# Storing dK, dV and o of an attention backward kernel in other pieces

## The chip, the cores and the metric

The kernel runs on one NeuronCore of a Trainium2 chip. Its engines are TensorE (PE in the profile), VectorE (DVE), ScalarE (ACT), GpSimd (POOL) and SyncE (SP), each with an instruction queue of its own, and sixteen DMA engines move data between the device memory and SBUF. The metric is the device time of one execution in microseconds (us), as the median of several runs. All times are of the whole kernel unless a part is named.

## The reference

Grouped query attention with its gradients, for 32 batches, 32 query heads of 4 positions, 4 key heads of 2048 positions and 128 elements, all bfloat16. The forward pass and its vector-Jacobian product are returned: o, dq, dk and dv.

```python
def _fwd_reference(q, k, v):
    B, Hq, Sq, D = q.shape
    Hkv = k.shape[1]
    rep = Hq // Hkv
    k = jnp.repeat(k, rep, axis=1)
    v = jnp.repeat(v, rep, axis=1)
    scale = D ** -0.5
    scores = jnp.einsum("bhqd,bhkd->bhqk", q, k) * scale
    p = _softmax(scores, axis=-1)
    return jnp.einsum("bhqk,bhkd->bhqd", p, v)

def reference(q, k, v, grad_out):
    ...
    _out, _vjp = jax.vjp(_f, q, k, v)
    _grads = _vjp(grad_out)
    _out0 = jnp.asarray(_out)
    return (_out0, *[jnp.asarray(_g) for _g in _grads])
```

For each batch k and v are 2 MB each and are read once; dk and dv are 2 MB each and are written once. o, dq, q and grad_out are 32 KB a batch.

## The kernel before

One batch is the unit of work. Its 32 query heads by 4 positions are 128 rows, which fill the 128 partitions, 32 rows for each of the four key heads. Key position 16p + c of a head lies in partition p at place c, so that each partition reads and writes 4 KB in one piece for each head.

The steps of a batch, by the names that the code uses in its order lists:

- LK and LV load k and v, four DMAs of 512 KB each, on SP's queue (lines 154 and 160). Every fourth batch LK also loads q and grad_out for the next four batches, two DMAs of 128 KB, on POOL's queue (line 142, `GROUP`).
- KT and VT transpose k and v on PE (line 181), DVE copies the result out of PSUM (line 183). QDT does the same for q and grad_out.
- Sa and Sb are the scores (line 198) with their row maximum on DVE (line 211). EXa and EXb are the exponentials on ACT (line 222).
- NRM makes the reciprocal of the row sums, and POOL scales grad_out and q by it into the tiles dop and qp, eight small instructions (line 231).
- ET and dST transpose the exponentials and the score gradients (lines 248 and 250). dPa and dPb are the gradient of the probabilities (DVE, line 338).
- O and dQ gather their product over all keys in PSUM (line 264). DVE scales o (line 274) into an o tile, which is stored from POOL's queue (line 276); DVE then reads the tile again for delta (line 279). ACT scales dq (line 288), and POOL's queue stores it (line 290).
- dV and dK are outer products, eight pieces each. PE makes a piece (line 303), ACT copies it into the 2 MB tile of its batch (line 307), and after the eighth piece POOL's queue stores the tile in two DMAs of 1 MB, heads 0 and 1 and then heads 2 and 3 (line 326). The last batch is stored in halves of the keys instead, one after every four pieces (line 319).

The order of all steps is written out by hand (`HEAD`, `STEADY` and `TAIL`): steps of neighbouring batches are interleaved, `dV7@3` being piece 7 of dV of batch 3. The order holds for each engine's queue: an instruction that waits holds all behind it on its engine. In one round of `STEADY` POOL meets, in this order: dop and qp of the batch (in NRM), the store of dq of the batch before, the store of dk of the batch before, the store of o, every fourth batch the two loads for q and grad_out, and the store of dv.

Tiles come from pools with a fixed number of buffers, and a step that takes a buffer waits until the work on its last content has ended. The pools that matter here: `k_pool` 3 and `v_pool` 2 batches, `out_pool` 4 tiles shared by dk and dv, `io_pool` 3 buffers each for the o tile and the dq tile.

Of the kernel before, what the change touches and what calls it, by code (L numbers as in the profile page):

```python
# [9 lines left out]
BF16 = mybir.dt.bfloat16  # L10
ACT = mybir.ActivationFunctionType
ALU = mybir.AluOpType
# [69 lines left out]
def kernel(ctx: ExitStack, tc: tile.TileContext, q, k, v, grad_out, out_0, out_1, out_2, out_3):  # L82
    nc = tc.nc
    B, Hq, Sq, D = q.shape
    NH, Sk = k.shape[1], k.shape[2]
    P = 128
# [3 lines left out]
    scale = float(D) ** -0.5  # L90
# [11 lines left out]
    ds_pool = ctx.enter_context(tc.tile_pool(name="dsp", bufs=2))  # L102
    dst_pool = ctx.enter_context(tc.tile_pool(name="dstp", bufs=2))
    out_pool = ctx.enter_context(tc.tile_pool(name="outp", bufs=4))
    io_pool = ctx.enter_context(tc.tile_pool(name="iop", bufs=3))
    qd_pool = ctx.enter_context(tc.tile_pool(name="qdp", bufs=2))
    sm_pool = ctx.enter_context(tc.tile_pool(name="smp", bufs=3))
    ps_pool = ctx.enter_context(tc.tile_pool(name="ps", bufs=1, space=bass.MemoryType.PSUM))
# [16 lines left out]
    o_f = out_0.rearrange("b h s d -> b (h s) d")  # L125
# [6 lines left out]
    store = nc.gpsimd  # L132
    st = {}
# [125 lines left out]
    def gathered(S, xt, kv):  # L259
        t = banks.take(1)  # L260
        ps = banks.ap(t)[:, 0, 0:D]
        for c in range(C):
            for h in range(NH):
                nc.tensor.matmul(  # L264
                    ps[G * h:G * h + G, :], lhsT=S[f"{xt}{c // 8}"][:, c % 8, G * h:G * h + G], rhs=S[kv][:, h, c, :],
                    start=(c == 0), stop=(c == C - 1), tile_position=(0, G * h),
                )
        return t, ps

    def O(b):  # L270
        S = st[b]
        t, ps = gathered(S, "et", "v")
        o_sb = io_pool.tile([P, D], BF16, name="o_sb")
        nc.vector.tensor_scalar(out=o_sb[:], in0=ps, scalar1=S["rinv"][:], scalar2=None, op0=ALU.mult)
        banks.give(t)
        store.dma_start(out=o_f[b], in_=o_sb[:])
        junk = sm_pool.tile([P, D], BF16, name="junk")
        S["delta"] = sm_pool.tile([P, 1], FP32, name="delta")
        nc.vector.tensor_tensor_reduce(
            out=junk[:], in0=o_sb[:], in1=S["do"], scale=1.0, scalar=0.0,  # L280
            op0=ALU.mult, op1=ALU.add, accum_out=S["delta"][:],
        )

# [8 lines left out]
    def outer(S, x, y, dst, name, i, b, copy):  # L292

        if name not in S:
            S[name + "left"] = 8
            S[name] = out_pool.tile([P, NH, C, D], BF16, name=name, tag="outp")
        t = banks.take(2)
        ps = banks.ap(t).rearrange("p a (j c d) -> p a j c d", j=2, c=2)
        for c in range(2):
            u = P * ((2 * i + c) % 8)  # L300
            for a in range(2):
                r = slice(2 * G * a, 2 * G * a + 2 * G)
                nc.tensor.matmul(  # L303
                    ps[:, a, :, c, :], lhsT=S[f"{x}{i // 4}"][r, u:u + P], rhs=S[y][r, :, :],
                    start=True, stop=True, tile_position=(2 * G * a, 0),
                )
        copy(  # L307
            out=S[name][:, :, 2 * i:2 * i + 2, :].rearrange("p h c d -> p h (c d)"),
            in_=banks.ap(t).rearrange("p a (j w) -> p (a j) w", j=2),
        )  # L310
        banks.give(t)
        S[name + "left"] -= 1
        if b == B - 1:

            half = f"{name}half{i // 4}"
            S[half] = S.get(half, 4) - 1
            if S[half] == 0:
                c = slice(8 * (i // 4), 8 * (i // 4) + 8)
                store.dma_start(
                    out=dst[b].rearrange("p h (c d) -> p h c d", d=D)[:, :, c, :].rearrange("p h c d -> p h (c d)"),  # L320
                    in_=S[name][:, :, c, :].rearrange("p h c d -> p h (c d)"),
                )
        elif S[name + "left"] == 0:
            o = S.pop(name)
            for a in range(2):
                store.dma_start(out=dst[b][:, 2 * a:2 * a + 2, :], in_=o[:, 2 * a:2 * a + 2].rearrange("p h c d -> p h (c d)"))  # L326

    def dV(b, i, copy=nc.scalar.copy):
        outer(st[b], "e", "dop", dv_v, "dv", i, b, copy)

    def dK(b, i, copy=nc.scalar.copy):
        outer(st[b], "ds", "qp", dk_v, "dk", i, b, copy)

    def dP(b, i):
# [6 lines left out]
        banks.give(t)  # L341

    table = {"LK": LK, "LV": LV, "QDT": QDT, "O": O, "dQ": dQ, "NRM": NRM}
    for i, c in enumerate("ab"):
        for n, f in (("S", S_), ("EX", EX), ("dP", dP), ("ET", ET), ("dST", dST)):
# [8 lines left out]
    for w in STEADY.split():  # L354
        ahead = 0
        for mark, n in (("+3", 3), ("+2", 2), ("+", 1), ("-2", -2), ("-", -1)):
            if w.endswith(mark):
                w, ahead = w[:-len(mark)], n
# [3 lines left out]
    with tc.manual_schedule():  # L362

        for w in HEAD.split():
            w, b = w.split("@")
# [5 lines left out]
        for w in TAIL.split():  # L371
            w, b = w.split("@")
# [31 lines left out]
```

## Time and profile before

| what | value |
|---|---|
| time, median of 3 runs | 699.42 us (697.81 to 702.17) |
| the profiled execution, its own time | 698.71 us |
| its span from first to last instruction | 696.7 us |
| mean granted TensorE clock | 0.98 |
| PE busy | 626.0 us, 90% |
| DVE busy | 584.5 us, 84% |
| ACT busy | 569.1 us, 82% |
| POOL busy | 302.7 us, 43% |
| moved by DMA | 274.44 MB, mean 394 GB/s |
| dv, dk stores | 64 and 64 DMAs of 1 MB, 23.6 and 22.1 us from issue to landing (median) |
| o, dq stores | 32 and 32 DMAs of 32 KB, 23.2 and 16.2 us |
| k, v loads | 128 and 128 DMAs of 512 KB, 13.8 and 18.6 us |

The page of a profile describes one execution, so its sums are made against that execution's own time. A share of busy time is a mean over the whole span. The DMA row gives for each fortieth of the span the mean busy share of the sixteen DMA engines in tenths, so that a 9 can be anything from 90% on. The chain of waits follows the work back from the last instruction to what released it, at every step; the table of waits sums the time in which an engine stood still, by what ended it. A DMA has landed when all sixteen DMA engines have marked their share of it as done, and what waits for a DMA waits for the last of these marks.

### The profile page before, as it was taken

The numbers are of one execution on the slowest core, as the hardware profiler recorded it, in microseconds if no ns is written. First come the engines' busy times: TensorE is split into PE (matmuls) and PEld (weight loads), VectorE is DVE, ScalarE is ACT, GpSimd is POOL, SyncE is SP. The second block draws the span as 40 slices with busy tenths as digits, with TensorE's granted clock in tenths as the row PEclk, the third lists the DMA queues.
The fourth block names the chain that finished last, engine by engine and source line by source line (L and its number), as shares of the span: only waits on it lengthen the run. The fifth ranks groups of instructions, "written<-read, shape, count | busy, mean of one in ns | idle before, by whom it ended". The sixth has DMA issues, their size and how long they took to land.

```text
span 696.7 us, 28064 instructions
## 1 busy us (share of the span) xinstructions
PE 626.0 (90%) x12352; PEld 454.1 (65%) x12352; DVE 584.5 (84%) x992; ACT 569.1 (82%) x673; POOL 302.7 (43%) x506
## 2 busy tenths in 40 slices
PE   5899999999998989979999798998998889998982
PEld 4577776677676656666666676667766677666661
DVE  5999999999997998869988688888988869898960
ACT  0698989899887989869888687887888868888994
POOL 1355443555454435443354424544434543345452
PEclk9999999999999999999999899999999989999997
DMA  9989999999999999999999999999999999999767
GB/s 339 400 317 411 417 415 416 416 413 415 417 415 417 414 417 416 417 409 412 415 415 413 373 397 398 400 410 382 416 416 417 415 340 393 415 414 415 289 257 274
DMA packets 75577, 274.44 MB, mean 394 GB/s; under 512 B 8448, under 2 KB 8448, under 8 KB 75456
## 3 DMA queue, kind: packets, MB, share of 16 engines
q0 software_dynamic: 37536, 138.16, 49.3%
q1 hardware_dynamic: 37920, 134.50, 48.9%
q8 instruction: 96, 1.57, 0.8%
q14 instruction: 25, 0.20, 0.1%
HBM read 136.31 MB, written 136.31 MB: 391 GB/s over the span
## 4 chain that ended last, share of the span: by engine, by line
PE 43%; DMA 33%; ACT 6%; DVE 5%; POOL 5%; issue 5%; SPq 0%; POOLq 0%; DVEq 0%; ACTq 0%
PE banks L181 18%; DMA k_sb<-in_k_dram 15%; DMA out_dram<-dk 12%; PE banks L303 10%; PE banks L264 7%; ACT dv L307 5%; PE banks L248 5%; DMA out_dram<-dv 4%; PE banks L198 3%; POOL dop L231 2%; DMA v_sb<-in_v_dram 2%; DVE kt L183 2%; DVE ds L338 1%; ACT dk L307 1%; POOL qp L231 1%
## 5 line engine op out<-in xcount | busy, mean ns | idle before, releaser
L307 ACT CAST dv<-banks 128x1024 bf16<-128x1024 f32 x256 | 245.5, 1028 | 56.9 <-PE banks L303 56.3
L307 ACT CAST dk<-banks 128x1024 bf16<-128x1024 f32 x256 | 250.7, 1025 | 34.5 <-PE banks L303 23.6
L183 DVE COPY kt<-banks 128x1024 bf16<-128x1024 bf16 x256 | 164.3, 680 | 8.3 <-PE banks L181 8.3
L183 DVE COPY vt<-banks 128x1024 bf16<-128x1024 bf16 x256 | 166.2, 680 | 1.3 <-PE banks L181 0.9
L181 PE MATMUL banks<-ident,k_sb 128*128 128x128 bf16 x2048 | 145.8, 221 | 13.1 <-DMA k_sb<-in_k_dram 8.6
L181 PE MATMUL banks<-ident,v_sb 128*128 128x128 bf16 x2048 | 143.5, 220 | 14.3 <-ACT dv L307 9.7
L231 POOL TENSOR_SCALAR dop<-do_sb,rinv 32x128 bf16<-32x128 bf16 x128 | 76.7, 599 | 181.3 <-PE banks L303 118.9
L181 PEld LDWEIGHTS <-k_sb 128*128 128x128 bf16 x2048 | 120.8, 99 | 41.9 <-issue 31.7
L181 PEld LDWEIGHTS <-v_sb 128*128 128x128 bf16 x2048 | 122.2, 98 | 28.7 <-issue 23.3
L303 PE MATMUL banks<-dop,e 64*128 64x256 bf16 x1024 | 99.3, 276 | 15.1 <-POOL dop L231 11.3
L326 POOL DMA_DIRECT2D out_dram<-dv x62 | 43.7, 709 | 138.0 <-ACT dv L307 67.6
L338 DVE SCALAR_TENSOR_TENSOR ds<-banks,delta,e 128x1024 bf16<-128x1024 f32 x64 | 82.2, 1284 | 17.3 <-PE banks L198 14.3
L303 PE MATMUL banks<-qp,ds 64*128 64x256 bf16 x1024 | 86.4, 272 | 2.1 <-ACT dk L307 1.4
L231 POOL TENSOR_SCALAR qp<-q_sb,srinv 32x128 bf16<-32x128 bf16 x128 | 78.1, 610 | 10.7
L222 ACT ACTIVATE e<-banks,negb 128x1024 bf16<-128x1024 f32 x64 | 70.7, 1111 | 8.6 <-DVE negb L214 8.5
L211 DVE TENSOR_REDUCE m<-banks 128x1 f32<-128x1024 f32 x64 | 75.1, 1215 | 0.9 <-PE banks L198 0.9
L303 PEld LDWEIGHTS <-e 64*128 64x128 bf16 x1024 | 34.0, 94 | 63.1 <-issue 46.7
L250 DVE COPY et<-banks 128x1024 bf16<-128x1024 bf16 x64 | 41.3, 686 | 29.6 <-PE banks L248 29.6
L303 PEld LDWEIGHTS <-ds 64*128 64x128 bf16 x1024 | 42.2, 94 | 28.8 <-ACT dv L307 13.1
L326 POOL DMA_DIRECT2D out_dram<-dk x62 | 44.0, 713 | 13.6 <-DMA out_dram<-dk 13.0
L250 DVE COPY dst<-banks 128x1024 bf16<-128x1024 bf16 x64 | 43.5, 681 | 5.5 <-PE banks L248 3.6
L248 PE MATMUL banks<-ident,ds 128*128 128x128 bf16 x512 | 39.4, 221 | 7.1 <-ACT dk L307 6.8
(39 smaller groups left out, 484.1 us busy)
## 6 DMA issues: line engine op xcount, KB each, us to landing
k_sb<-in_k_dram SPq DMA_DIRECT2D x128, 512.0 KB, 13.8
v_sb<-in_v_dram SPq DMA_DIRECT2D x128, 512.0 KB, 18.6
out_dram<-dv POOLq DMA_DIRECT2D x64, 1024.0 KB, 23.6
out_dram<-dk POOLq DMA_DIRECT2D x64, 1024.0 KB, 22.1
out_dram<-o_sb POOLq DMA_DIRECT2D x32, 32.0 KB, 23.2
out_dram<-dq_sb POOLq DMA_DIRECT2D x32, 32.0 KB, 16.2
q_sb<-in_q_dram POOLq DMA_DIRECT2D x7, 128.0 KB, 21.9
do_sb<-in_grad_out_dram POOLq DMA_DIRECT2D x7, 128.0 KB, 22.0
```

Of the source, the lines that this page charges most:

```text
L181: nc.tensor.transpose(out=ps[:, 4 * hh + j, :], in_=S[which][:, 2 * (i % 2) + hh, 4 * (i // 2) + j, :], identity=ident[:])
L183: nc.vector.tensor_copy(out=S[f"{which}t{i}"][:], in_=ps)
L211: nc.vector.reduce_max(out=S["m"][:, i:i + 1], in_=S[f"s{i}"][1], axis=AX.X)
L222: nc.scalar.activation(out=S[f"e{i}"][:], in_=ps, func=ACT.Exp, bias=S["negb"][:], scale=scale, accum_out=S["l"][:, i:i + 1],)
L231: nc.gpsimd.tensor_scalar(out=t[r, h % 2, :], in0=src[r, :], scalar1=by[r, :], scalar2=None, op0=ALU.mult)
L248: nc.tensor.transpose(out=ps[:, u, :], in_=S[f"{src}{i}"][:, P * u:P * u + P], identity=ident[:])
L250: nc.vector.tensor_copy(out=S[f"{name}{i}"][:], in_=ps)
L264: nc.tensor.matmul(ps[G * h:G * h + G, :], lhsT=S[f"{xt}{c // 8}"][:, c % 8, G * h:G * h + G], rhs=S[kv][:, h, c, :], start=(c == 0), stop ...
L303: nc.tensor.matmul(ps[:, a, :, c, :], lhsT=S[f"{x}{i // 4}"][r, u:u + P], rhs=S[y][r, :, :], start=True, stop=True, tile_position=(2 * G * ...
L307: copy(out=S[name][:, :, 2 * i:2 * i + 2, :].rearrange("p h c d -> p h (c d)"), in_=banks.ap(t).rearrange("p a (j w) -> p (a j) w", j=2),)
L326: store.dma_start(out=dst[b][:, 2 * a:2 * a + 2, :], in_=o[:, 2 * a:2 * a + 2].rearrange("p h c d -> p h (c d)"))
L338: nc.vector.scalar_tensor_tensor(out=S[f"ds{i}"][:], in0=ps, scalar=S["delta"][:], in1=S[f"e{i}"][:], op0=ALU.subtract, op1=ALU.mult,)
```

## The change

Five edits, all on stores that POOL issues:

- dk and dv of a batch are stored in one DMA of 2 MB instead of two of 1 MB. The last batch is stored as before.
- dv of batches 3, 7, 11 and so on to 27 is stored in two DMAs instead, partitions 0 to 119 and 120 to 127.
- The o tile holds two batches, and both are stored together after the second one. The pairs that end with batch 7, 11 and so on to 31 are stored in two DMAs, partitions 0 to 103 and 104 to 127.
- The pair of batches 0 and 1 is stored in three DMAs: partitions 8 to 127 of batch 0, partitions 8 to 127 of batch 1, and partitions 0 to 7 of both.
- `io_pool` has 2 buffers instead of 3: two o tiles of two batches each, and two dq tiles.

Bytes, arithmetic and the order of the steps stay.

```diff
-    io_pool = ctx.enter_context(tc.tile_pool(name="iop", bufs=3))
+    io_pool = ctx.enter_context(tc.tile_pool(name="iop", bufs=2))
...
     def O(b):
         S = st[b]
         t, ps = gathered(S, "et", "v")
-        o_sb = io_pool.tile([P, D], BF16, name="o_sb")
-        nc.vector.tensor_scalar(out=o_sb[:], in0=ps, scalar1=S["rinv"][:], scalar2=None, op0=ALU.mult)
-        banks.give(t)
-        store.dma_start(out=o_f[b], in_=o_sb[:])
+        if b % 2 == 0:
+            st["o"] = io_pool.tile([P, 2, D], BF16, name="o_sb")
+        o_sb = st["o"][:, b % 2, :]
+        nc.vector.tensor_scalar(out=o_sb, in0=ps, scalar1=S["rinv"][:], scalar2=None, op0=ALU.mult)
+        banks.give(t)
+        if b == 1:
+            for w in range(2):
+                store.dma_start(out=o_f[w, 8:P], in_=st["o"][8:P, w])
+        if b % 2:
+            for r in (slice(0, 8),) if b == 1 else (slice(0, 104), slice(104, P)) if b % 4 == 3 and b > 3 else (slice(0, P),):
+                store.dma_start(out=o_f[b - 1:b + 1, r].rearrange("w p d -> p w d"), in_=st["o"][r])
...
         elif S[name + "left"] == 0:
-            o = S.pop(name)
-            for a in range(2):
-                store.dma_start(out=dst[b][:, 2 * a:2 * a + 2, :], in_=o[:, 2 * a:2 * a + 2].rearrange("p h c d -> p h (c d)"))
+            o = S.pop(name)[:].rearrange("p h c d -> p h (c d)")
+            for r in (slice(0, 120), slice(120, P)) if name == "dv" and b % 4 == 3 else (slice(0, P),):
+                store.dma_start(out=dst[b][r], in_=o[r])
```

## The prediction, made before the result was known

> **What bounds the kernel now.** I read the page's slices first, then the queues, then the chain of waits in 178 to 290 us, then the waits of POOL, then the landing records of single transfers.
>
> The page's second and third part (forty slices of 17.4 us; then each queue's share of sixteen engines' time):
>
> ```profile
> DMA  9989999999999999999999999999999999999767
> GB/s 339 400 317 411 417 415 416 416 413 415 417 415 417 414 417 416 417 409 412 415 415 413 373 397 398 400 410 382 416 416 417 415 340 393 415 414 415 289 257 274
> ...
> q0 software_dynamic: 37536, 138.16, 49.3%
> q1 hardware_dynamic: 37920, 134.50, 48.9%
> ```
>
> The DMA engines are full from the second slice to slice 37, and stores (q0, from POOL) and loads (q1, from SP) take half each. PE is busy 90% of the span, but it isn't what a batch waits for, as the chain shows (start, us, what):
>
> ```profile
> 199.03 0.03 SPq L154
> 199.06 0.04 issue
> 199.11 16.95 DMA k_sb<-in_k_dram
> ...
> 220.24 16.81 DMA k_sb<-in_k_dram
> ...
> 241.24 17.01 DMA k_sb<-in_k_dram
> ```
>
> A batch takes 21.1 us here, and 17 of them are one k load. The o product (line 274) gives the batches' times: 26.6 us for batch 0, 203.8 for batch 9, 672.9 for batch 31. That is 19.7 us a batch while the stores' backlog grows, which is the engines' own pace, and 469.1/22 = 21.3 after it, which is DMA's.
>
> Which DMA engine, no page says, but each transfer records sixteen landing marks, one for each DMA engine. Sorted, they give the spread:
>
> | transfer | first to 7th | 8th to 15th | 16th |
> |---|---|---|---|
> | dv, issued 113.2 | 127.9 to 130.4 | 130.5 to 132.3 | 134.2 |
> | dk, 269.3 | 282.4 to 284.5 | 288.2 to 290.4 | 296.1 |
> | dv, 622.6 | 631.7 to 632.5 | 632.5 to 633.9 | 653.2 |
>
> One engine is 13 to 20 us behind all others, and every wait on a transfer is a wait for it. Its packets are seen alone at 674.4 to 675.0 us, when the others have run dry: 172, 160, 176, 160 ns for 4 KB, a start every 163.5 ns. The usual packet takes 159 and starts every 155. Each engine carries 272.6 MB/16/4 KB = 4160 packets; by the marks, the late engine does 3643 from 60 to 660 us, one per 164.7 ns. So it never rests, and its work is the kernel's time. Eight others trail the best seven by 6 us at 290. I put that down to the 96 instruction blocks of 16 KB (q8, 948 ns, and the packet behind each takes 441 instead of 159: 1.2 us each, 12 on each of eight).
>
> **Part 1: dK, dV as one 2 MB transfer.** 62 POOL issues of 0.71 us go, 44 us, less what a 2 MB issue costs above a 1 MB one (0 to 0.71 us each, so 0 to 44 us of POOL's time; I take a quarter, as a load of 512 pieces is issued in 0.75). Nothing rests on it: POOL is busy 43%, and its idle time before dop is waiting for PE:
>
> ```profile
> POOL dop L231 <- PE banks L303: 118.9, 20, 6.6
> POOL out_dram L326 <- ACT dv L307: 67.6, 20, 5.1
> ...
> POOL out_dram L326 <- DMA out_dram<-dk: 35.1, 10, 4.4
> POOL out_dram L326 <- DMA out_dram<-dv: 22.1, 6, 4.2
> POOL q_sb L142 <- DMA out_dram<-dk: 17.4, 5, 4.1
> ```
>
> The last three are POOL waiting for the landing of the eighth transfer before (its marks go round eight semaphores): dv at 561.45 follows a dv landing at 560.9. Four batches now hold 26 POOL transfers, then 18, so eight reach back 1.8 batches instead of 1.2, 37 us against a longest landing of 31. With 4.3 us ahead of o these make 79 us, and they go. They are worth 0 in the sum, as the late engine works through all of them; what is late next is the out tile (four of them, two batches), whose dv evacuation on ACT then waits for the same late engine. The bytes and 4 KB packets stay; 62 fewer marks of 9 ns on every engine are 0.4 us off.
>
> **Part 2: dV of batches 3, 7, ... 27 as 120 and 8 rows** (31 is the last and goes in halves). No row shows how a transfer of 120 rows is dealt to sixteen engines. If eight rows go to each of fifteen, one engine is left out: it saves 8 rows of 4 packets, 32, and the 8 row piece gives up to 4 back. 28 to 32 packets by 164.7 ns are 4.6 to 5.3 us, seven times 32 to 37 us. Eight engines get one row more: 4 by 155 ns, 0.62 us, seven times 4.3 us.
>
> If the left-out engine is the late one, it gains more than it needs: it lost 4.5 us on the eight between 128 and 300 us (2.2 to 6.7), 2.6%, so 16 us over 620 us. Then the eight set the end, 16 earlier, less the 4.3 of added rows: 12 us. By batches: 130 packets by 155 ns are 20.15, the instruction blocks 14.4/32 = 0.45, the rows 0.13, together 20.7 against 21.3; 0.6 by 22 batches is 13 us. PE's 19.7 lies below both, so the engines don't take over. I take 12; the ends are 6 (if the tail from 656 us on gives some of it back) and 18 (no added row on the eight).
>
> [...]
>
> **Part 3: o for two batches, every second pair as 104 and 24 rows; the pair of batches 0 and 1 as 120, 120 and 8.** 64 KB are 4 KB for each engine: an uneven deal moves under 0.2 us each time, 7 times, 1 us. Sixteen issues of 0.56 us go and nine to ten come back. The pieces matter only if they shift where the next 120 rows start. Two o tiles of two batches cover 80 us against a landing of at most 26, two dq tiles 41 us against 19: no wait. Batch 1 gets two more issues, 1.1 us on POOL ahead of dop: 0 to 1 us, I take 0.
>
> Sum against this execution's 698.7 us (span 696.7 and 2.0 around it): 698.7 - 12 - 0.4 = 686.3. The median of the runs, 699.4, lies 0.7 higher: 687.
>
> **Rivals.**
> *Another engine is left out, or the rows are dealt evenly.* The late one keeps its 4160 packets, and parts 1 and 3 save what it doesn't wait for: 699. If it is one of the eight with a row more, 28 by 164.7 ns make 4.6: 703.5. For it: no row ties the left-out engine to the late one, and a deal whose start wanders would hit it once in sixteen times. Against it: the late engine's excess over the best is (164.7 - 155) by 4160 packets, 40 us, and seven reliefs of one engine are 32 to 37, so the cut has the size of just this shortage, which it has for nothing else in the profile. That is a judgement and not a proof, and I give it 0.26 against 0.60 for the forecast. [...]
> *Slower: the 120 row pieces run badly.* [...] Up to double, 32 packets by 159 ns are 5.1 us, seven times 36 us: 722 with the late engine relieved. It decides from packets a third longer (12/36); 1% slower needs over half ((12 + 7)/36). For it: when stores run alone at 689 us packets take 169 to 173, and loads in the worst 5 us (480 us) 199 in the mean, so packets do stretch, by 6 to 25%. Against it: that falls short of a third. Chance 0.07.
> *Half a gain.* The late engine is relieved, but the load bursts of 390 to 480 us (means of 166 to 199 ns, about 12 us over the span) stay as the new limit: 692 to 697. Chance 0.07.
>
> **How the numbers follow.** Forecast 0.60, rivals 0.26, 0.07, 0.07. A measurement of this kernel tells 1%, 7 us. Faster (under 692.4): 0.57 of the forecast and 0.02 of the half gain, 0.59. Slower (over 706.4): 0.06 of the bad pieces and 0.02 of the missed engine, 0.08. Same: 0.33. The forecast alone lies in 681 to 693; the range goes on to 704 for the missed engine.
>
> **What would show it.** Right: the sixteenth mark within 6 us of the fifteenth everywhere, batches at 20.7 us after the tenth, no POOL wait on a landing, k loads of 10 to 13 us in the chain. Wrong engine: the sixteenth still 13 to 20 us late, batches at 21.3, POOL's waits turned into ACT's waits for dv's store. Bad pieces: GB/s drops after each fourth dV. The prediction fails if the left-out engine isn't the late one, or if a new engine trails once fifteen are left.

## The result, and the profile after

The change makes the kernel slower by one per cent. The median of 14 runs is 707.8 us (704.03 to 711.97) against 700.34 us (697.81 to 703.25) of the kernel before, measured beside it; the ratio is 1.010, its 95% interval 1.008 to 1.0119. The prediction had 687 us, with 681 to 693 for the forecast alone and on to 704 for a missed engine. The profiled execution took 708.14 us, with a span of 706.3. The ratios in this document leave out runs that lie over 1.5% above the fastest of their kernel, which the medians of e2 and e8 below include.

The page's second and third part of the changed kernel, columns as before (forty slices of 17.7 us; each queue's share of sixteen engines' time):

```profile
DMA  9999999999999999999999999999999999999767
GB/s 340 389 326 411 417 405 395 415 413 416 415 408 415 414 416 405 414 413 416 403 382 399 412 409 373 362 410 414 415 380 370 384 412 417 361 363 380 317 256 282
...
q0 software_dynamic: 36880, 138.16, 49.9%
q1 hardware_dynamic: 37920, 134.50, 48.3%
```

The engines are still full, and the bytes are the same, but of slices 4 to 37 nine are now under 390 GB/s, where three were before (373, 382 and 340): there are dips in slices 7, 21, 25, 26, 30, 31 and 35 to 37, where the 120 row pieces of dV land (about 112, 372, 460, 549 and 636 us), and smaller ones at 199 and 284. The engines stay busy there and move less, and packets are slower: between 60 and 640 us 907 of the 28,620 store packets of 4 KB took over 230 ns, against 148 of 28,574 before; the median of the 907 is 316, about twice the usual 159.

The chain of waits in the stretch that was shown of before, and one later on (start, us, what):

```profile
201.41 16.70 DMA k_sb<-in_k_dram
...
222.28 17.21 DMA k_sb<-in_k_dram
...
243.68 17.48 DMA k_sb<-in_k_dram
...
470.79 21.76 DMA v_sb<-in_v_dram
492.56 21.18 DMA v_sb<-in_v_dram
513.76 21.68 DMA v_sb<-in_v_dram
```

A batch still waits 17 us for one k load, and from 449 to 652 us the chain is one v load after another, up to 23.8 us each. By the o product the batches after the tenth take 21.7 us (206.1 to 682.7 us), where 21.3 became 20.7 in the forecast. The table of POOL's waits (engine and line, what ended the wait, sum, times, longest):

```profile
POOL dop L231 <- DVE rinv L239: 175.9, 22, 19.5
POOL out_dram L335 <- ACT dv L314: 143.3, 30, 9.7
POOL dop L231 <- PE banks L310: 67.6, 10, 7.0
```

The waits on the eighth transfer before are gone, as Part 1 said, and with them 38 us of POOL's busy time (302.7 to 264.5). Little was waiting for POOL (PE 11.3 us in all before, 1.3 after), and no gain came of it. The waits of ACT for the landing of dv that the prediction expected in their place don't appear either.

The landing marks show where the forecast went wrong. At the 120 row piece issued at 430.5 us the first mark comes at 436.9, the next 4.2 us later, the fifteenth 14.4 and the sixteenth 23.6 us later. At all seven pieces one engine, the one that is left out, is 3.7 to 6.0 us ahead of all others, where the whole dV stores have at most 2.3. The last is 0.1 to 2.4 us behind the fifteenth at the first three and 6.8 to 13.8 at the other four. The left-out engine isn't the late one.

### The profile page after: what moved, and what is told of

It reads as the page before. It is cut to its first block, busy times and chain, and to the rows that moved or that the text cites. A ratio compares the mean times of both kernels' runs of the same rounds, so it can differ in the third digit from the quotient of the medians.

```text
span 706.3 us, 27988 instructions
## 1 busy us (share of the span) xinstructions
PE 627.0 (89%) x12352; PEld 453.7 (64%) x12352; DVE 587.2 (83%) x992; ACT 569.0 (81%) x673; POOL 264.5 (37%) x444
## 4 chain that ended last, share of the span: by engine, by line
DMA 58%; PE 29%; DVE 4%; issue 2%; ACT 2%; POOL 2%; SPq 1%; POOLq 0%; DVEq 0%; ACTq 0%
DMA k_sb<-in_k_dram 30%; DMA v_sb<-in_v_dram 29%; PE banks L181 13%; PE banks L310 7%; PE banks L264 5%; PE banks L248 2%; PE banks L198 2%; ACT dv L314 2%; DVE kt L183 1%; DVE ds L347 1%; POOL dop L231 1%; DVE m L211 1%; DVE vt L183 1%; SPq L160 0%; POOL out_dram L326 0%
## 5 line engine op out<-in xcount | busy, mean ns | idle before, releaser
L183 DVE COPY kt<-banks 128x1024 bf16<-128x1024 bf16 x256 | 166.6, 684 | 23.5 <-PE banks L181 22.5
L181 PE MATMUL banks<-ident,k_sb 128*128 128x128 bf16 x2048 | 151.7, 225 | 35.4 <-DMA k_sb<-in_k_dram 29.0
L181 PEld LDWEIGHTS <-k_sb 128*128 128x128 bf16 x2048 | 124.3, 101 | 66.2 <-issue 33.5
L335 POOL DMA_DIRECT2D out_dram<-dv x38 | 27.6, 727 | 155.7 <-ACT dv L314 142.8
L198 PE MATMUL banks<-vt,qdt 128*32 128x512 bf16 x512 | 40.5, 388 | 0.8 <-issue 0.5
L198 PE MATMUL banks<-kt,qdt 128*32 128x512 bf16 x512 | 40.5, 390 | 0.6
```

What stands on the lines that cost most here:

```text
L181: nc.tensor.transpose(out=ps[:, 4 * hh + j, :], in_=S[which][:, 2 * (i % 2) + hh, 4 * (i // 2) + j, :], identity=ident[:])
L183: nc.vector.tensor_copy(out=S[f"{which}t{i}"][:], in_=ps)
L198: nc.tensor.matmul(ps[G * h:G * h + G, a, :], lhsT=S["qdt"][:, col, G * h:G * h + G], rhs=xt[:, 4 * (h % 2):4 * (h % 2) + 4, :].rearrange( ...
L335: store.dma_start(out=dst[b][r], in_=o[r])
```

## The experiments

Their edits are given against the changed kernel, or against the kernel without pieces (e1). "By the rule" means a count of starts, which is the author's assumption: a transfer of 128 rows moves nothing, and one that goes to fewer engines moves the start on by as many as it uses, zero following on fifteen. In e13 120 rows and 60 rows went to fifteen engines, 104 to thirteen, 24 to twelve, and 16, 32 and 64 to sixteen; for other numbers of rows the engines are assumed as well. e12 and e17 below fit the count: where it leaves out the late engine, the last mark moves by 5.6 us instead of 10.3 to 12.3 (e12), and by 2.9 instead of 5 to 7 at two stores sixteen apart (e17). The numbers of engines below are such counts, from zero at the start of the profiled execution; no view numbers the engines.

### Which part costs: e1, e4, e10

e1 takes all pieces away; e4 makes dV whole and keeps the pieces of o; e10 is the kernel before with 2 MB transfers and nothing else.

```diff
 # e1: each loop over pieces, and no pieces of batches 0 and 1
+for r in (slice(0, P),):
 # e4: the loop of dV alone
+for r in (slice(0, P),):
 # e10, in before.py
-for a in range(2):
-    store.dma_start(out=dst[b][:, 2 * a:2 * a + 2, :], in_=...)
+store.dma_start(out=dst[b], in_=o)
```

> dK, dV in one 2 MB transfer each and o in pairs, but every transfer over all 128 rows. Theory M (missed engine): the late DMA engine carries 4160 packets again instead of 4188, so 4.6 us less than the change and level with before, 699 to 702 us, the sixteenth landing mark 13 to 20 us late, no POOL wait on a landing. Theory P (the 120 row pieces run badly): the same time, and the packets over 230 ns vanish from the stores between 100 and 640 us. Rival T (the 2 MB transfers themselves cost): 706 to 708 us.

> As the change with all its pieces of o, but dV of every batch in one transfer of 128 rows. Theories M and P: 699 to 702 us, as without any pieces, since the pieces of o are 64 KB each. Rival O (the pieces of o cost, by POOL's issues or by engines left unequal): 703 to 708 us.

> The kernel before with dK and dV in single 2 MB transfers and nothing else: o for each batch, three buffers. Theory (the 2 MB transfers cost the 2 us by which the kernel without pieces lies over the kernel before): 702.3, ratio 1.003. Rival (the pairs of o and the two buffers cost it): 700.3, ratio 1.000. The prediction had 0.4 us less than before for it: 699.9.

e1: 702.26 us, ratio 1.0026 (1.0012 to 1.0039). e4: 702.88, 1.003 (1.0016 to 1.0045). e10: 701.0, 1.0008 (0.9989 to 1.0028). So the pieces of o cost nothing that shows, the pieces of dV cost some 5 us, and 2 MB transfers with o in pairs about 2, which e10 does not pin on either of the two.

### Where the deal starts: e2, e3, e9, e12

The start is moved, by the rule, by splitting o of batches 0 and 1 in another way: 28 and 100 rows in e2 (start 8, so that 7 is left out), none in e3 (start 0). e9 is e2 with the last dq split in the same way, so that one execution moves the start by 16. e12 is e1 with dV's pieces, so that the start wanders by 7.

```diff
 # e2; e3: (slice(0, P),) in its place
+for r in (slice(0, 28), slice(28, 128),) if b == 1 else (slice(0, 104), slice(104, P)) if ...
 # e9, besides
+for r in (slice(0, 28), slice(28, P)) if b == B - 1 else (slice(0, P),):
+    store.dma_start(out=dq_f[b, r], in_=dq_sb[r])
 # e12, in e1
+for r in (slice(0, 120), slice(120, P)) if name == "dv" and b % 4 == 3 else (slice(0, P),):
```

> [...]

> As the change, but o of batches 0 and 1 goes as one transfer of 128 rows, so that the next 120 rows start at zero and leave out number 15. Theory M: 685 to 692 us if that is the late engine, else it keeps all 4160 packets, and 28 more if it is among the first eight: 700 to 708 us. Theory P: 700 to 708 us either way.

> The start of the first 120 row deal is put 8 engines on (o of batches 0 and 1 as 28 and 100 rows: 14 and 10 engines), and the last dq, again as 28 and 100 rows, puts it back, so that the shifts of one execution add up to 16. Theory (the start goes on from one execution to the next, the left-out engine is the one before the start): all runs start alike, leave out engine 7, and lie within 2 us of each other, at the lower group of the kernel with start 8, 701 to 704; the two groups of that kernel, 701 to 707 and 706 to 712, are then starts 8 and 0. If 7 is the late engine and its relief is worth what the prediction said, 690, and the sixteenth mark within 6 us of the fifteenth. Rival (the start is the same in each execution anyway and the alternation was chance): the runs spread over 10 us again, 701 to 712.

> dV of every fourth batch as 120 and 8 rows, o in pairs of 128 rows, so that each split starts 7 engines further than the one before (starts 0, 7, 14, 5, 12, 3, 10) and the added rows fall on all engines nearly alike. Theory of the added rows (the late engine does 28 packets more, 4.6 us): now it gets some 12 to 16 of them, 2 to 2.6 us, so 704.5 over the 702.3 without pieces. Rival (the pieces' packets at double time, wherever they start): 707 to 708, as the changed kernel.

e2: 706.56 us (701.25 to 712.09), 1.0075 (1.0043 to 1.0107). e3: 710.4 (709.18 to 712.77), 1.0141 (1.0112 to 1.0171). e9: 704.64 (701.48 to 707.23), 1.0052 (1.0025 to 1.0079). e12: 709.7 (703.57 to 710.31), 1.0106 (1.0069 to 1.0143). No start that was tried gains. In e2 the runs alternate in the order of their taking: the first, third and so on have a mean of 710.1 us, the others of 704.3, which are the times of e3 (start 0) and e9 (start 8). That would fit a start that goes on from one execution to the next. It isn't shown: e9's runs still spread over 6 us where 2 were expected, and in the profiled execution of e2, one of the longer ones, the last mark moves by 0.62 to 0.86 us from the 120 to the 8 row piece at four of the seven cuts, as it does in e9 (start 8) and not in e3 (start 0). e12 came out above what was worked out for added rows alone (704.5) and nearer to its rival (707 to 708).

### A fair cut, and another queue: e5, e6, e7, e8

e5 cuts dV of every fourth batch into 64 and 64 rows; e6 stores all dK and dV from ACT's queue, uncut; e7 has the 120 and 8 rows from ACT's queue; e8 cuts every dV into 120 and 8. All in e1.

```diff
 # e5
+for r in (slice(0, 64), slice(64, P)) if name == "dv" and b % 4 == 3 else (slice(0, P),):
 # e6; e7 for the cut dV alone
+nc.scalar.dma_start(out=dst[b][r], in_=o[r])
 # e8
+for r in (slice(0, 120), slice(120, P)) if name == "dv" else (slice(0, P),):
```

> All stores over 128 rows, but dV of every fourth batch as rows 0 to 63 and 64 to 127: all sixteen engines keep equal shares (4 rows and 4 rows), and no engine is missed or favoured. [...]

> All stores over 128 rows; dK and dV in 2 MB transfers issued from ACT's queue instead of POOL's, o and dq still from POOL's. Theory L (one engine is late because of transfers that POOL issues): the sixteenth mark stays within 3 us of the fifteenth, the engines' pitch is 155 to 160 ns, and the time falls to 684 to 692 us. Rival (the late engine is slow by itself, or is slow whenever stores run): it stays 7 to 20 us late, and the time is 700 to 704 us, or more by ACT's issues (54 by 0.4 us, 22 us at most).

> [...]

> All o in one piece, dV of every batch but the last as 120 and 8 rows from POOL's queue: 31 splits in place of 7. By shares the start of a split moves by 7 of 16 each time, so that each engine is left out about twice. Theory P: its cost grows with the number of splits, from 5.5 us (the change against no pieces) to some 24 us: 720 to 730 us, with about four times as many store packets over 230 ns. Theory M: the late engine is left out in two of 31 splits and gets a row more in half of them, 15 by 0.66 less 2 by 5.3 us: 702 us within 3. The split at which the late engine's lag falls by 5 us tells its place.

e5: 703.3 us, 1.004 (1.0024 to 1.0055). e6: 706.24, 1.0088 (1.0059 to 1.0116). e7: 710.16, 1.0138 (1.011 to 1.0167). e8: 756.33, 1.0645 (1.0563 to 1.0726). In e5, where none of the sixteen engines is left out or favoured (64 rows went to all of them in e13), 640 store packets are over 230 ns against e1's 395, and the time is about 1 us over e1's, within the intervals. In e6 one engine still trails (6.4 us behind the fifteenth at the v loads from 320 to 640 us, in the median), so its lateness isn't made by the large stores of POOL's queue. Why e6 is slower wasn't followed. e8's times spread from 740.8 to 773.3 us, far over the 720 to 730 expected. By the ratios it costs 43 us over e1 for 31 cuts, 1.4 us each, where seven cost 0.8 each: the price of a cut grows where every dV is cut.

### The pieces by themselves: e11, e13

After the last batch, with the engines idle but for the last stores, rows of one dV tile are stored, each group after the one before has landed.

```diff
 # e11: (128), (120, 8), (120, 8), (128, 128), (120, 8, 128), and the last again with k loads beside it
 # e13
+for q, lo, hi in ((store, 0, 128), (store, 0, 120), (store, 8, 128), (store, 0, 64), (store, 32, 96), ...):
+    nc.gpsimd.memset(o[:, 0, 0:1], 0.0)
+    x, b = next(n)
+    q.dma_start(out=x[b][lo:hi], in_=o[lo:hi])
```

> The pieces measured by themselves: stores of dK and dV of batches 26 to 30 are left out, and after the last batch its dV tile is stored six times, each once the one before has landed: 128 rows; 120 and 8; 120 and 8 again (7 engines further by the rule of the start); 128 and 128; 120, 8 and 128; the same with four k loads of 512 KB beside it. Its time is not to be compared. [...] Rival (only a backlog makes them slow): 160 to 172 ns in all groups that stand alone, and packets over 230 ns only in the last two groups, where an engine that is ahead works beside others that are behind. Marks: with 120 rows alone one mark comes about 5 us ahead of the fifteen others.

> Stores of dK and dV of batches 24 to 30 are left out; after the last batch rows of its dV tile are stored in thirteen DMAs, each once the one before has landed. Its time is not to be compared. [...] Rival (a smaller or uneven transfer is slow by itself): rows 32 to 95 take what rows 0 to 63 take. [...]

In e11 all three groups with 120 rows and no loads are slow, at starts 0, 7 and 14: 14 engines run at 295 to 325 ns a packet, and a single one at 159. The two times 128 rows stay at 164 in the median. So neither a backlog nor a certain start is needed. With k loads beside them (the last group) only 14 of 535 store packets took over 230 ns from 758 to 768 us: beside loads most of the slowness is gone. Why, no run shows. In e13 the same number of rows is fast or slow by where it lies. The view of DMA in two stretches, first that of rows 0 to 63, then that of rows 32 to 95 (GB/s in fortieths of the stretch; the last line has the time from issue to landing):

```profile
GB/s 0 0 0 0 0 0 0 0 0 224 202 269 180 202 247 135 292 112 269 224 180 269 135 269 157 224 202 180 292 112 269 202 180 202 224 269 23 0 0 0
...
out_dram<-dv POOLq DMA_DIRECT2D x1, 1024.0 KB, 6.7
```

```profile
GB/s 0 0 0 0 0 0 0 0 0 0 0 0 0 244 383 418 418 453 349 453 418 418 349 453 383 418 383 383 418 349 418 383 488 349 453 140 0 0 0 0
...
out_dram<-dv POOLq DMA_DIRECT2D x1, 1024.0 KB, 4.3
```

About 200 GB/s against 400, for the same megabyte in sixteen equal shares. The table has all thirteen; the columns are the engines by their marks or the packets by their duration:

| rows, queue | fast, 156 to 172 ns | about 305 ns | about 610 ns |
|---|---|---|---|
| 0 to 127 | all, but 23 of 949 packets, counted with the stores ahead of it | | |
| 0 to 119 and 8 to 127 | one engine | 14 engines | |
| 0 to 63; 0 to 31 | | all | |
| 32 to 95 | all | | |
| 0 to 103 | 3 engines | 10 engines | |
| 104 to 127 | | 12 engines | |
| 0 to 15 | | | all |
| 32 to 91 | 15 engines | | |
| ACT: 0 to 119 | one engine | 14 engines | |
| ACT: 0 to 63 / 32 to 95 | none / all | all / none | |

So 64 rows from row 0 on took about 305 ns a packet on all engines, and 64 rows from row 32 on 156 to 172; 16 rows from row 0 on took about 610. 120 rows were slow on 14 engines whether they began at row 0 or at row 8, with a single one at 159 ns, while 60 rows from row 32 on were fast on all fifteen and 128 rows on all sixteen. What the slow engines have in common no view shows: the runs tell which rows are slow when they are stored together, and not why.

### Which engine is late, and what its relief is worth: e14 to e18

Rows 32 to 95 kept 156 to 172 ns a packet in e13, so pieces of them can relieve an engine without slowing the packets. e14 stores rows 32 to 95 twice in every fourth dV; e15 and e16 store rows 32 to 91 and row 92 instead, from start 8 (7 is left out) and start 0 (15). e17 has rows 32 to 91 once in every dV, so that the left-out engine goes round. e18 stores all of dV again, and o is cut so that by the rule each 60 row piece starts at 5.

```diff
 # e14
+for r, w in ((slice(32, 96), slice(0, 64)), (slice(32, 96), slice(64, P))) if name == "dv" and b % 4 == 3 else ...
+    store.dma_start(out=dst[b][w], in_=o[r])
 # e15, e16: (32, 92), (92, 93), twice; e17: (32, 92), (32, 96) in each dV
 # e18, in e1
+u = {1: 40, 3: P, 29: P, 31: 28}.get(b, 120 if b % 4 == 1 else 108)
+for r in (slice(0, u), slice(u, P)) if u < P else (slice(0, P),):
...
+for u, w in ((32, 92), (92, 96), (0, 32), (96, P)) if name == "dv" and b % 4 == 3 else ((0, P),):
+    store.dma_start(out=dst[b][u:w], in_=o[u:w])
```

> dV of every fourth batch is stored as its rows 32 to 95 twice, to both halves of the destination; rows 0 to 31 and 96 to 127 are left out. [...] Rival (two shares of a transfer are slow by themselves): 704 to 708.

> As the kernel with rows 32 to 95 twice, but each time as rows 32 to 91 on fifteen engines and row 92 on one, rows 93 to 95 left out; by the rule of the start the two together move the start by 16, and o of batches 0 and 1 puts it at 8 (the last dq puts it back), so engine 7 is left out 14 times and gets one row back: 24 packets less each time, 168 in all, 27.7 us at 164.7 ns. If 7 is the late engine and the prediction's gain was there to be had, 690 (686 to 695), the sixteenth mark within 6 us of the fifteenth. If it isn't, or if a new engine trails at once, 702.3. [...]

> [...] If 15 is the late engine and its relief is worth what the prediction said, 690 (686 to 695); if the late engine is another, 702.3 (701.5 to 703.5). With the kernel of start 8 it tells which of the two the late engine is, or that neither is.

> Each dV (but the last) is stored as its rows 32 to 91 on fifteen engines and its rows 32 to 95 on sixteen; rows 0 to 31 and 96 to 127 are left out. By the rule of the start it goes back by one with each batch, so that the left-out engines are 15, 14, 13 ... 0 and then 15 to 1 again. At each 60 row store the left-out engine's mark comes some 2 to 3 us ahead of the others; only where it is the late engine that is left out, its early mark is missing, and the sixteenth mark stays 8 to 15 us behind. Theory of one fixed late engine: the early mark is missing in two stores that lie sixteen batches apart (or in one after batch 9 and its match before, where the lateness is still small), which gives its number. Rival (whichever engine falls behind stays behind, or the lateness moves): the early mark is missing at places that are not sixteen apart, or nowhere, or the lateness is below 6 us throughout, since the reliefs go round. Time, either way, near 700, as each engine is relieved alike.

> The kernel without pieces, and dV of every fourth batch as rows 32 to 91 on fifteen engines, row 92 to 95 on four, 0 to 31 and 96 to 127 on sixteen; o in such pieces (40 and 88, 120 and 8, 108 and 20, 28 and 100 rows) that each 60 row store starts at engine 5 by the rule, so that 4 is left out seven times, and that one execution moves the start by a multiple of 16. Engine 4 does 16 packets less and gets 4 back, 84 in all, 13.8 us at 164.7 ns; 5, 6 and 7 do 28 more. [...] Theory (the late engine's work is the time, as the prediction had it): it led the fifteenth by 7 to 12 us without pieces, so 10 us less than 702.3 plus 0.5: 692 to 693 (689 to 697), the sixteenth mark within 6 us of the fifteenth in the second half. Rival (the engines share a limit, and the late one only comes last): 701 to 704.

e14: 701.34 us, 1.0022 (1.0005 to 1.0039), with 360 store packets over 230 ns against e1's 395: these pieces cost nothing that shows. e15: 698.99, 0.9971 (0.9953 to 0.9989). e16: 699.06, 0.9974 (0.9948 to 1.0). Both gain 2.3 us on e14 and neither gains 12; in both one engine stays behind, 5 to 15 us after the fifteenth at the dV stores from 320 to 640 us. So by the count the late one is neither 7 nor 15. Why both gain 2.3 us is open; they store 42 rows less, 0.7 MB of 272.6, a quarter of a per cent.

e17 (695.7 us, one run, with some 0.75% of the packets left out) gives the number. From the dK store ahead to the 60 row piece, the sixteenth mark of store 11 to 14 and 27 to 29 (counted from one) moves on by:

| store | 11 | 12 | 13 | 14 | ... | 27 | 28 | 29 |
|---|---|---|---|---|---|---|---|---|
| left out, by the rule | 5 | 4 | 3 | 2 | | 5 | 4 | 3 |
| sixteenth mark moves, us | 4.98 | 2.88 | 4.95 | 7.01 | | 5.03 | 2.91 | 5.40 |

Sixteen store packets and as many of the loads are some 5 us, by an estimate from 155 to 164.7 ns for each. At all stores from 4 to 30 but numbers 12 and 28, sixteen apart, the last engine does them; there it does only the loads. One fixed engine is late, and by the rule it is number 4. (The last store, at the end of the span, is as short for want of loads.) The sign that was expected, a missing early mark, doesn't tell the two apart from the rest: the second mark follows within 0.5 us of the first at ten other stores too.

The same marks now read the other runs. From the 120 to the 8 row piece the sixteenth moves by 0.62 to 0.78 us in the changed kernel after the first piece (start 6: the rows added go to 5 to 12), by 1.25 to 1.83 in e3 (15 and 0 to 6, so 4 among them), by 0.65 to 0.85 in e9 (7 to 14, after the first), and in e12 by 1.35, 0.84, 1.69, 1.45, 0.75, 1.3 and 0.67, where the rule has 4 among them in the first, third, fourth and sixth. All agree. In e7 it moves by 1.33 to 1.49, as where 4 has a row more; where ACT's queue starts, no view shows. e12 holds a further one: at its fourth cut the rule leaves out 4 itself, and over this 120 row piece the sixteenth mark moves by 5.6 us, where it moves by 10.3 to 12.3 at the other six.

e18 relieves number 4: **691.7 us** (688.79 to 695.01) against 700.17 beside it, ratio 0.9879 (0.9853 to 0.9906). It stores everything, and it is faster than both kernels, than the one before by 1.2%. Its page, second to fourth part (the last line is the chain's share by engine):

```profile
DMA  9989999999999999999999999999999999999857
GB/s 338 404 305 406 416 416 416 415 414 416 415 415 415 413 417 415 416 415 415 416 414 414 414 417 412 396 395 411 416 412 393 414 414 416 414 411 401 336 235 272
...
q0 software_dynamic: 37376, 138.17, 49.8%
q1 hardware_dynamic: 37920, 134.50, 48.8%
...
PE 69%; issue 8%; DMA 8%; ACT 5%; DVE 4%; POOL 4%; SPq 0%; POOLq 0%; ACTq 0%; DVEq 0%
```

And the same line of the changed kernel, then of the kernel before:

```profile
DMA 58%; PE 29%; DVE 4%; issue 2%; ACT 2%; POOL 2%; SPq 1%; POOLq 0%; DVEq 0%; ACTq 0%
...
PE 43%; DMA 33%; ACT 6%; DVE 5%; POOL 5%; issue 5%; SPq 0%; POOLq 0%; DVEq 0%; ACTq 0%
```

The dips are gone, and the chain runs over PE, with 8% of DMA instead of 58% in the changed kernel and 33% before. The sixteenth mark lies 1.0 us (median) behind the fifteenth at the stores, and the batches after the tenth take 21.0 us.

## Why the prediction was wrong

**The step that failed** is Part 2's "if the left-out engine is the late one". It was given 0.60 on the ground that the cut has the size of the late engine's shortage. By the count the left-out engine was number 5 in the profiled execution, and the late one is number 4: one beside it. What stood in for a proof of the aim was a match of sizes, 32 to 37 us against 40: a sound reason for what a cut can do, as e18 shows, and none for where it falls. It also put the lateness too high: 13 to 20 us behind all others holds at the large stores only from about 410 us on, and there for dv's; its own table has 2 and 6 us in the first two rows.

**The size behind the if is borne out, by another cut.** 12 us (6 to 18) was worked out for relieving the late engine; e18 takes 84 packets or 13.8 us of it away and gains 10.6 us on e1 (702.3 to 691.7, on another chip; 10.3 by the ratios). Of the 692 to 693 expected for it, 0.5 us for the rows outside 32 to 95 is an estimate that no run shows apart: half of the 1 us by which e5 lies over e1. e16 takes 27.7 us away from number 15 and gains 2.3 on e14. So the late engine's work was what set the time. The batches came to 21.0 us, 20.7 was said. What comes next wasn't as said: the prediction had eight DMA engines as the next limit and no limit from the compute engines, and the chain of e18 runs over PE. Whether 120 and 8 rows, aimed at number 4, would have gained 12 us with their slow packets, no run shows.

**The first rival was right on where the relief falls, and its price was too low.** It had 699, or 703.5 with a row more on the late engine. The row more seems to cost: e3 and e7, where by the marks it falls on the late engine in each cut, are at 1.0141 and 1.0138, e9, where it never does, at 1.0052: 0.89% or 6.2 us, for which 4.6 was worked out (e7 also issues from ACT). In the changed kernel the starts would go on by 6 in each execution (15 + 15 + 8 less two sixteens), if they are carried over, and number 4 would get the rows in half of them; the mean of e3's and e9's ratios is 1.0097, the measured one 1.010. No run shows it apart, and two things speak against it: the profiled execution, with its rows on 5 to 12, took 708.14 us all the same, and e12, for which the added rows alone were worked out to give 704.5, has a median of 709.7. How the 5 us of the dV pieces divide between added rows and slow packets stays open.

**The second rival's slow packets are there, in a smaller dose.** It had packets up to double and 36 us at most. Nothing in the profile of before shows the double; e13 has about 305 ns against 159. Its sign, GB/s dropping after each fourth dV, came. Alone, the packets of 14 of 15 engines take that long, but with loads beside them most of it goes: e9, with seven such pieces and no added rows on number 4, is 1.0052 against e1's 1.0026, about 1.8 us, and e5 is 1.004; their intervals overlap e1's. In e8, with 31 pieces, it no longer hides. What spoke against it, that packets stretch by 6 to 25% and no more, was read from 128 row transfers, which run at 156 to 172 ns alone (e13), so it was no evidence on pieces of 120.

**Part 1** gave 0.4 us of gain. (62 marks of 9 ns are 0.56 us; the difference is too small to measure.) e1, which has it and o in pairs, is slower by 0.26% (1.8 us), and e10, which has it alone, can't be told from before. No gain is there; the sign of what is left is open. POOL's waits went as was said, and were worth the 0 that the sum gave them.

**Part 3** at 0 was right: the pieces of o make e4 and e1 differ by 0.6 us, and o in pairs, with its two buffers, makes e1 and e10 differ by 1.3, both within the intervals.

## What to carry to other kernels

When one DMA engine is late by its landing marks, a cut of a few stores can give it less to do, but the cut has to be aimed: pass the left-out place round all engines in one run, read where the last mark jumps less, and only then fix the start, for relieving the wrong engine gained 2.3 us at most here. Take the piece that relieves from partitions 32 to 95, and not from row 0: as many rows took 3.1 us there and 5.5 from row 0 (e13). A match between the size of a change and the size of a shortage is no evidence that the change reaches it.

## What the runs showed of the hardware

- From the first packet to the last mark a store of 120 rows alone takes 9.9 us (e13), where 128 rows take 5.8 (e11): fewer bytes, 1.7 times the time. Rows 0 to 63 take 5.5 us, rows 32 to 95, as many, 3.1 (e13). ACT's queue shows nearly the same numbers as POOL's (10.2, 5.5 and 3.2).
- The same packet of 4 KB took about 610 ns in a store of rows 0 to 15, about 305 in rows 0 to 31, 0 to 63 and 104 to 127, and 156 to 172 in rows 32 to 91 and 32 to 95 (e13).
- One DMA engine of sixteen does a packet every 164.7 ns in the mean, by its marks in the kernel before, where the others start one every 155. By the count it is number 4; the marks agree on each of the three chips that ran e3, e9, e12 and e17, and its relief was run on a fourth (e18). In e6, with no cuts to number it by, one engine trails as well, so the large stores of POOL's queue aren't the cause. What the cause is wasn't found.
- Runs of the kernel e2 taken in turn differ by 6 us in the mean (710.1 and 704.3). Whether the place in the round of engines where a transfer starts outlasts an execution stays open.
